# KV transposed by DMA, one weight load split in two, and half-width ones matmuls, in a fused adaLN, linear attention and GEGLU kernel

## The chip, the core and the metric

The kernel runs on one core of a Trainium2 chip. The metric is the device time of one execution in microseconds. Seven of the fast runs show a mean granted clock of TensorE of 0.998 in place of 1.000. A second number is used throughout: the span of one profiled execution and the stretches inside it, which the trace gives to 0.01 us.

Engine names: PE is TensorE (matmuls), PEld its weight loads, DVE is VectorE, ACT is ScalarE, SPq is the queue of SyncE, from which almost all loads and stores are issued.

## The reference, cut to what matters

```python
mod = silu(c) @ w_mod                  # six rows of 1024: sa, ca, ga, sb, cb, gb
h   = layernorm(x) * (1 + ca) + sa     # x: 2048 tokens x 1024
q, k, v = h @ wqkv                     # 32 heads of 32
pq, pk  = phi(q), phi(k)               # phi(t) = (t > 0 ? t + 1 : exp(t)) + 1e-6
kv  = pk^T v  per head                 # 32 x 32
o   = (pq @ kv) / (pq . sum(pk))
x   = x + ga * (o @ wo)
h   = layernorm(x) * (1 + cb) + sb
x   = x + gb * (gelu(h @ w_gate) * (h @ w_up)) @ w_down
```

The kernel never forms `o`. It multiplies KV by wo first (called W2 below), scales pq by the reciprocal of the denominator, and multiplies the scaled pq by W2.

## The kernel before

Four heads form a group, so KV is eight masked blocks of 128x128 (`KVBD`). The product with wo needs each block transposed as the stationary operand: eight PE transposes into PSUM bank 4, then a copy by ScalarE.

```python
def kvt():
    for g in range(NG):                                    # NG = 8
        e.transpose(PS16(4, g*P, (g+1)*P), KVBD[:, g, :], IDENT)    # PE
    e.activation(KVT, PS16(4), Copy)                                # ACT

def w2_pair(g, b0=2):                  # one wo product: two matmuls, banks b0 and b0 + 1
    for half in range(2):
        e.matmul(PS(b0 + half), KVT[:, g, :], WO[:, g, half*512:(half+1)*512])
    e.activation(W2[:, g, :], both banks, Copy)
```

A Q block is eight matmuls of 512 columns into one PSUM bank. Its bank is free once `phi` is through with it: ScalarE takes the exponential, VectorE does two more passes, the last of which ("pq addition") reads the bank again.

```python
def phi(bank, dst):
    e.activation(EB, PS(bank), Exp)                        # ACT
    e.tensor_scalar(EB, EB, 1.0, 1e-6, min, add)           # DVE
    e.scalar_tensor_tensor(dst, PS(bank), 0.0, EB, max, add)   # DVE: the pq addition

def q_next():
    b = (0, 1, 2, 3)[n] if n < 4 else n % 2                # n counts these Q blocks
    q_block(..., b)

den(0, 3)          # denominators; DVE: add, reciprocal; store to DRAM
rb_load(0); rb_load(1)   # 16 loads that spread the reciprocals over the partitions ("rb")
kvbd()             # DVE masks KV
q_next(); q_next()
for u in range(8):
    q_next()
    if u == 0: kvt()
    else:      w2_pair(u - 1)
    if u in (3, 4): pq_scale(0, 0, GH[u - 3])    # DVE: pq times rb, first half of the tokens
    if u in (6, 7): pq_scale(0, 1, GH[u - 6])
w2_pair(7, 4)
# ... then 12 wo chunks (pq times W2), the FFN
```

The rows of `mod` that vary along the free dimension are made by matmuls with a stationary operand of ones, 32 columns wide. Row j lands in partitions 32j to 32j+31:

```python
for h in range(2):                     # high and low half of the value
    for j in range(n):                 # n = 2 or 4 rows of 512
        e.matmul(ps_all[32*j:32*(j+1), bank], ONES, src(k0 + j, h))
```

At the start, the first 25 us, loads of x, of four quarters of w_mod ("wmq") and of wk arrive in turns. A quarter of w_mod has to be multiplied before the k matmuls of the matching two 128-row pieces of wk can use their input. wk's second quarter comes in one load, the third and fourth in two each.

Of the kernel before, what the change touches and what calls it, by code (L numbers as in the profile page):

```python
# [7 lines left out]
ACTF = mybir.ActivationFunctionType  # L8
ALU = mybir.AluOpType

P = 128
# [7 lines left out]
NG = 8  # L19
# [195 lines left out]
def bass_adaLN_cond__linear_attn_block__geglu_ffn__prompt_kernel(  # L215
# [13 lines left out]
    scr_row = nc.dram_tensor("scr_row", [3, 4, 512], f32).ap()  # L229
    scr_rd = nc.dram_tensor("scr_rd", [NSG, 2, HPG, NG * (SGW // 2)], f32).ap()  # L230
    with ExitStack() as es:
# [3 lines left out]
        ps_all = es.enter_context(nc.psum_tensor("ps_all", [P, 8 * 512], f32))  # L235
        ps16 = ps_all.bitcast(bf16)

        def at(name, shape, dty, off):
            return nc.alloc_sbuf_tensor_at(name, shape, dty, offset=ABASE + off, align_bytes=4)
# [45 lines left out]
        KVBD = at("kvbd", [P, NG, P], bf16, OFF_ROW)  # L285
        KVT = at("kvt", [P, NG, P], bf16, OFF_ROW + 2048)
# [22 lines left out]
        IDENT, BMASK, BM32, Z32 = (_small[k] for k in ("ident", "bmask", "bm32", "z32"))  # L309
        RDC = _small["rdc"]  # L310
        ONES, SILF, C8, CT, CHALF, THC, SILUT = (_small[k] for k in ("ones", "silf", "c8", "cT", "chalf", "thc", "siluT"))
# [5 lines left out]
        def r_sm(name):  # L317
            return [(SMO[name], SMO[name] + SMSZ[name], name)]
# [68 lines left out]
        def r_kvbd(g0, g1):  # L387
            return [(OFF_ROW + g0 * 256, OFF_ROW + g1 * 256, "kvbd")]

        R_KVT = [(OFF_ROW + 2048, OFF_ROW + 4096, "kvt")]  # L390

        def pr(b):
            return [(b * 2048, (b + 1) * 2048)]
# [4 lines left out]
        def PS16(b, c0=0, c1=1024):  # L398
            return ps16[:, b * 1024 + c0: b * 1024 + c1]

        sch = Sched()
        T, A, V, G, Q = PE_, ACT_, DVE_, POOL_, SP_
# [11 lines left out]
        def pset_writer(b, o):  # L414
            for t_ in pr(b):
                sch.ps.set_writer(t_[0], t_[1], o)
# [30 lines left out]
        def w_dma(dst, off, name, kind, c0, c1, dc0=0, dc1=NDC):  # L447
            return sch.dma(Q, lambda e: e.dma_start(dst[:, dc0:dc1, c0:c1], wqkv_v[:, dc0:dc1, kind * D + c0:kind * D + c1]),  # L448
                           wr=[t_ for dc in range(dc0, dc1) for t_ in r_w(off, name, dc, c0, c1)], note=f"{name}.{dc0}.{c0}")

        def wmq_dma(q, ts=(0, 1)):
            for t in ts:
                sch.dma(Q, lambda e, t=t: e.dma_start(WMQ[q][:, :, t, :], wm_v[:, :, t * D + q * 256:t * D + (q + 1) * 256]),  # L453
                        wr=r_wmq(q, t), note=f"wmq{q}.{t}")
# [10 lines left out]
        x_dma(3, 4)  # L465
        for q in range(1, 4):
            wmq_dma(q)
            for d0, d1 in ((2, 4),) if q == 1 else ((2 * q, 2 * q + 1), (2 * q + 1, 2 * q + 2)):
                w_dma(WK, OFF_WK, "wk", 1, 0, D, d0, d1)
        w_dma(WV, OFF_WV, "wv", 2, 0, 512, 0, 4)  # L470
        w_dma(WV, OFF_WV, "wv", 2, 0, 512, 4, 8)
# [7 lines left out]
               rd=r_sm("c8") + r_sm("ident"), pwr=pr(4))  # L479
# [4 lines left out]
               rd=r_sm("thc") + r_sm("chalf"), wr=r_sm("siluT"))  # L484
# [68 lines left out]
        def tdma(stream, dst, src, rng, wr_, note):  # L553
            d_ = [last_t[0]] if last_t[0] is not None and last_t[0].stream != stream else []
            last_t[0] = sch.dma(stream, lambda e: e.dma_start_transpose(out=dst, in_=src), rd=rng, wr=wr_, deps=d_, note=note)
# [81 lines left out]
        def mod_rows(parts):  # L637
            for k0, n, bank, src in parts:
                o = None
                for h in range(2):  # L640
                    for j in range(n):
                        ap, rng = src(k0 + j, h)
                        o = sch.op(T, lambda e, h=h, j=j, ap=ap, bank=bank: e.matmul(  # L643
                            ps_all[32 * j:32 * (j + 1), bank * 512:(bank + 1) * 512], ONES[:, :], ap, start=(h == 0), stop=(h == 1)),
                            rd=rng + r_sm("ones"), pwr=(pr(bank) if h == j == 0 else ()), note=f"modr{k0}.{h}.{j}")
                pset_writer(bank, o)

        def mod_store(n, bank, dst, rng, row):
            sch.op(A, lambda e: e.activation(dst[0:32 * n, :], ps_all[0:32 * n, bank * 512:(bank + 1) * 512], ACTF.Copy),
                   prd=pr(bank), wr=rng, note=f"mrow{row}")  # L650
            return sch.dma(Q, lambda e: e.dma_start(scr_row[row, 0:n, :], dst[0:32 * n:32, :]), rd=rng, note=f"mrow{row}.st")

        def hl_src(k, h):
            return HL[k // 4][:, k % 4, h, :], r_hl(k, h, h + 1)
# [184 lines left out]
        for c_ in range(4):  # L839
            for vc, jg in (((0, 0), (1, 0)), ((0, 1), (1, 1)), ((2, 0), (2, 1)), ((3, 0), (3, 1)))[c_]:  # L840
                b = nb()
# [58 lines left out]
        for c_ in range(4, NCH):  # L900
# [23 lines left out]
            for jg in range(2):  # L924
                b = nb()
# [3 lines left out]
            for jg in range(2):  # L929
                b = nb()  # L930
# [3 lines left out]
            if c_ == 13:  # L934
# [6 lines left out]
                for dst, nt, a0 in ((SBT, "sbT", 0), (CBT, "cbT", 2)):  # L941
                    sch.dma(Q, lambda e, dst=dst, a0=a0: e.dma_start(dst[:, :], scr_row[1, a0:a0 + 2, :].rearrange("a (b p) -> p (a b)", p=P)),
                            wr=r_sm(nt), deps=[o_r], note=nt)
# [13 lines left out]
        def kvbd():  # L957
            for kb, gs in ((5, [0, 1, 2]), (6, [3, 4, 5]), (7, [6, 7])):
                n = len(gs)
                src = ps_all[:, kb * 512: kb * 512 + n * KV_SLOT].rearrange("p (a b) -> p a b", a=n)[:, :, 0:P]  # L960
                sch.op(V, lambda e, src=src, gs=gs, n=n: e.tensor_tensor(
                    KVBD[:, gs[0]:gs[0] + n, :], src, BMASK[:, :].unsqueeze(1).to_broadcast([P, n, P]), ALU.mult),
                    prd=pr(kb), rd=r_sm("bmask"), wr=r_kvbd(gs[0], gs[0] + n), note=f"kvbd{kb}")

        def kvt():
            for g in range(NG):
                sch.op(T, lambda e, g=g: e.transpose(PS16(4, g * P, (g + 1) * P), KVBD[:, g, :], IDENT[:, :]),
                       rd=r_kvbd(g, g + 1) + r_sm("ident"), pwr=pr(4), note=f"kvT{g}")
            sch.op(A, lambda e: e.activation(KVT[:].rearrange("p a b -> p (a b)"), PS16(4), ACTF.Copy), prd=pr(4), wr=R_KVT, note="kvt")

        def w2_pair(g, b0=2):
            for half in range(2):
                b = b0 + half
                sch.op(T, lambda e, b=b, half=half: e.matmul(PS(b), KVT[:, g, :], WO[:, g, half * 512:(half + 1) * 512], start=True, stop=True),  # L974
                       rd=R_KVT + [(OFF_WS + g * 2048 + half * 1024, OFF_WS + g * 2048 + (half + 1) * 1024, "wo")], pwr=pr(b), note=f"w2 {g}.{half}")
            sch.op(A, lambda e: e.activation(W2[:, g, :], ps_all[:, b0 * 512:(b0 + 2) * 512], ACTF.Copy),
                   prd=pr(b0) + pr(b0 + 1), wr=r_w(OFF_WK, "w2", g), note=f"w2cp{g}")
# [3 lines left out]
        def den(pr_, b):  # L981
            o = None
            for g in range(NG):
                for i in range(4):
                    sg, t0 = 2 * pr_ + i // 2, (i % 2) * HW
                    o = sch.op(T, lambda e, g=g, i=i, sg=sg, t0=t0: e.matmul(  # L986
                        ps_all[32 * i:32 * (i + 1), b * 512:b * 512 + HW], Z32[:, g, :], PQ[sg][:, g, t0:t0 + HW],
                        start=(g == 0), stop=(g == NG - 1)),
                        rd=r_sm("z32") + r_pq(sg, g, g + 1, t0, t0 + HW), pwr=(pr(b) if g == 0 else ()), note=f"den{pr_} {g}.{i}")
            pset_writer(b, o)  # L990
            sch.op(V, lambda e: e.tensor_scalar(RDC[:, :], PS(b, 0, HW), 1e-6, None, op0=ALU.add), prd=pr(b), wr=r_sm("rdc"), note=f"dene{pr_}")
            sch.op(V, lambda e: e.reciprocal(RDC[:, :], RDC[:, :]), rd=r_sm("rdc"), wr=r_sm("rdc"), note=f"rden{pr_}")
            o_s = sch.dma(Q, lambda e: e.dma_start(scr_rd[2 * pr_:2 * pr_ + 2].rearrange("s f k (g t) -> (s f k g) t", g=NG), RDC[:, :]),
                          rd=r_sm("rdc"), note=f"rden{pr_}.st")
            o_rd[pr_] = o_s
# [4 lines left out]
        def rb_load(sg):  # L1000
            i = sg % 2
            for h in range(2):
                made = []
                for k in range(HPG):
                    made.append(sch.dma(Q, lambda e, h=h, k=k: e.dma_start(
                        RB[i][32 * k:32 * (k + 1), h, :, :].rearrange("p a b -> p (a b)"),
                        scr_rd[sg, h, k:k + 1, :].to_broadcast([32, NG * HW])),
                        wr=r_rb(i, h) if k == 0 else (), deps=made[0].deps if k else [o_rd[sg // 2]], note=f"rb{sg}.{h}.{k}"))
                rb_ops[sg, h] = made
# [24 lines left out]
        q_evac(*first_q)  # L1034
        q_next()
        den(0, 3)
        rb_load(0)
        rb_load(1)
        kvbd()
        q_next()  # L1040
        q_next()
        for u in range(NG):
            q_next()
            if u == 0:
                kvt()
            else:
                w2_pair(u - 1)
            if u in (3, 4):
                pq_scale(0, 0, GH[u - 3])
            if u in (6, 7):  # L1050
                pq_scale(0, 1, GH[u - 6])
# [265 lines left out]
```

## Time and profile before

| | before |
|---|---|
| time, median of 6 runs beside the changed kernel | 838.81 us (837.82 to 840.23) |
| span of the profiled run | 835.7 us |
| PE busy | 829.8 us |
| waits of PE after the first 31 us | none |

The page of the profile, first the busy time of PE and then the chain that ended last, by engine:

```profile
PE 829.8 (99%) x4189; PEld 384.2 (46%) x4189; DVE 512.3 (61%) x898; ACT 336.2 (40%) x555; POOL 36.7 (4%) x91
...
PE 97%; SPq 2%; DMA 1%; issue 0%; DVE 0%
```

PE's waits over the whole span (line that waited, what it waited for, us in total, times, longest). All three lie in the first 25 us:

```profile
PE ps_all L478 <- POOL bmask L429: 2.1, 1, 2.1
PE ps_all L602 <- DMA wmq<-in_w_mod_dram: 0.6, 2, 0.4
PE ps_all L680 <- DVE h1T L565: 0.5, 1, 0.5
```

The chain of work that ended last, in order of time (start, us, what). L602 is the product that reads the last wmq quarter, L643 the ones matmuls, L986 the denominators, L721 Q blocks, L967 the KV transposes, L974 wo products, L1072 the wo chunks, L1157 the FFN's last matmuls:

```profile
24.78 0.95 PE ps_all L602 x32
...
151.80 0.97 PE ps_all L643 x12
...
173.68 0.99 PE ps_all L986 x32
174.67 5.29 PE ps_all L721 x24
179.96 0.45 PE ps_all L967 x8
180.40 1.73 PE ps_all L721 x8
182.13 0.43 PE ps_all L974 x2
182.56 1.73 PE ps_all L721 x8
...
195.94 3.45 PE ps_all L1072 x16
...
348.98 0.54 PE ps_all L643 x4
349.52 48.45 PE ps_all L1157 x224
...
784.75 48.50 PE ps_all L1157 x280
```

Read it as a ledger. From 24.78 us to the end, each piece begins where the one before it ends, so every microsecond taken off PE there is a microsecond of span, unless PE then meets a wait. The candidates of this change are the 0.45 us of transposes and the two sets of ones matmuls, 0.97 and 0.54 us. One Q block is 1.73 us, one wo product 0.43. VectorE starts the first scaling with the spread reciprocals at 188.24 us.

Two lines of the timeline of VectorE show how near other waits are. The columns are start, us, engine, line, operation, out<-in, forms:

```profile
181.37 0.69 DVE L672 SCALAR_TENSOR_TENSOR pq<-ps_all,eb 128x512 bf16<-128x512 f32 x1
...
188.24 1.28 DVE L1018 TENSOR_TENSOR pq<-pq,rb 128x512 bf16<-128x512 bf16 x2
```

The first is the pq addition that frees bank 0 at 182.06 us; the Q block that writes bank 0 next starts at 182.56 in the chain: half a microsecond of slack. The second is the first scaling with the spread reciprocals.

### The profile page before, as it was taken

What the parts mean: (1) busy time and instruction counts of PE and PEld (TensorE: products, weight loads), DVE (VectorE), ACT (ScalarE), POOL (GpSimd) and SP (SyncE); (2) the same over time, 40 slices, a digit from 0 to 9 for tenths busy, and PEclk for the clock granted to TensorE, in tenths of its full rate; (3) what the DMA queues carried; (4) which work ended last, traced back from release to release, by engine and by line L of the source; (5) the groups of instructions that cost most, each with busy time, mean ns of one, the idle gap of its engine ahead of it and who ended that gap; (6) DMA issues with size and microseconds to landing.
All of it is one profiled execution on the core that took longest, in us unless ns stands there. A gap on an engine that the chain in (4) does not pass through costs nothing.

```text
span 835.7 us, 11352 instructions
## 1 busy us (share of the span) xinstructions
PE 829.8 (99%) x4189; PEld 384.2 (46%) x4189; DVE 512.3 (61%) x898; ACT 336.2 (40%) x555; POOL 36.7 (4%) x91
## 2 busy tenths in 40 slices
PE   8999999999999999999999999999999999999998
PEld 4544444444444444444444444444444444444445
DVE  6778877687785567753566665355556535555512
ACT  2357777446423354420444442045554104455300
POOL 2012111000200000000000000000000000000000
PEclk9999999999999999999999999999999999999999
DMA  9984323239796779180555533055553305555000
GB/s 284 332 240 120 83 76 84 70 88 227 151 234 194 227 210 275 26 188 26 158 151 151 152 101 75 20 158 152 151 151 102 76 20 161 153 154 143 7 19 26
DMA packets 184102, 113.22 MB, mean 135 GB/s; under 512 B 35560, under 2 KB 175080, under 8 KB 183024
## 3 DMA queue, kind: packets, MB, share of 16 engines
q1 hardware_dynamic: 184032, 112.50, 49.9%
q8 instruction: 33, 0.54, 0.3%
q14 instruction: 21, 0.17, 0.1%
q10 hardware_dynamic: 16, 0.00, 0.0%
HBM read 100.67 MB, written 4.47 MB: 126 GB/s over the span
## 4 chain that ended last, share of the span: by engine, by line
PE 97%; SPq 2%; DMA 1%; issue 0%; DVE 0%
PE ps_all L1157 23%; PE ps_all L1129 23%; PE ps_all L1132 23%; PE ps_all L680 12%; PE ps_all L1072 7%; PE ps_all L721 7%; SPq L448 1%; PE ps_all L702 1%; SPq L453 1%; DMA wmq<-in_w_mod_dram 1%; PE ps_all L974 0%; PE ps_all L986 0%; SPq L442 0%; PE ps_all L643 0%; PE ps_all L756 0%; PE ps_all L602 0%
## 5 line engine op out<-in xcount | busy, mean ns | idle before, releaser
L1129 PE MATMUL ps_all<-h2T,wg 128*128 128x512 bf16 x896 | 339.6, 379 | 0.0
L1132 PE MATMUL ps_all<-h2T,wu 128*128 128x512 bf16 x896 | 339.6, 379 | 0.0
L1157 PE MATMUL ps_all<-wd,yT 128*128 128x512 bf16 (+3 forms) x952 | 194.2, 366 | 0.0
L1140 ACT ACTIVATE q<-ps_all 128x512 f32<-128x512 f32 x112 | 66.9, 597 | 226.1 <-PE ps_all L1129 222.2
L1157 PEld LDWEIGHTS ps_all<-wd,yT 128*128 128x128 bf16 x952 | 90.1, 98 | 103.9 <-issue 0.4
L1129 PEld LDWEIGHTS ps_all<-h2T,wg 128*128 128x128 bf16 x896 | 87.7, 98 | 105.8 <-issue 0.2
L1132 PEld LDWEIGHTS ps_all<-h2T,wu 128*128 128x128 bf16 x896 | 87.7, 98 | 105.6
L1145 DVE SCALAR_TENSOR_TENSOR ww<-th,guh 128x512 f32<-128x512 f32 x112 | 77.5, 692 | 77.9 <-ACT th L1144 77.9
L1142 DVE SCALAR_TENSOR_TENSOR ww<-q,ps_all 128x512 f32<-128x512 f32 x112 | 76.9, 687 | 77.5 <-ACT guh L1141 77.5
L1144 ACT ACTIVATE th<-ww 128x512 f32<-128x512 f32 x112 | 70.5, 629 | 87.4 <-DVE ww L1142 87.4
L1162 DVE TENSOR_TENSOR ps_all<-ps_all,gbb 128x512 f32<-128x512 f32 (+3 forms) x34 | 22.7, 667 | 94.8 <-PE ps_all L1157 94.8
L1147 DVE TENSOR_TENSOR yT<-ww,ps_all 128x512 bf16<-128x512 f32 x112 | 76.9, 686 | 3.8
L1141 ACT ACTIVATE guh<-ps_all 128x512 f32<-128x512 f32 x112 | 66.2, 591 | 0.0
L721 PE MATMUL ps_all<-h1T,wq 128*128 128x512 bf16 x256 | 58.7, 379 | 0.0
L680 PE MATMUL ps_all<-wv,h1T 128*128 128x512 bf16 x256 | 57.7, 379 | 0.0
L669 ACT ACTIVATE eb<-ps_all 128x512 f32<-128x512 f32 x64 | 37.5, 599 | 49.7 <-PE ps_all L721 22.1
L680 PE MATMUL ps_all<-wk,h1T 128*128 128x512 bf16 x248 | 56.6, 379 | 0.5 <-DVE h1T L565 0.5
L1072 PE MATMUL ps_all<-w,pq 128*128 128x512 bf16 x256 | 56.2, 379 | 0.0
L670 DVE TENSOR_SCALAR eb<-eb 128x512 f32<-128x512 f32 x64 | 27.1, 424 | 26.4 <-ACT eb L669 26.0
L1072 PEld LDWEIGHTS ps_all<-w,pq 128*128 128x128 bf16 x256 | 25.0, 98 | 30.2 <-issue 0.2
L680 PEld LDWEIGHTS ps_all<-wv,h1T 128*128 128x128 bf16 x256 | 24.9, 98 | 29.5
L680 PEld LDWEIGHTS ps_all<-wk,h1T 128*128 128x128 bf16 x248 | 23.8, 98 | 28.8 <-DVE h1T L565 1.6
(96 smaller groups left out, 479.7 us busy)
## 6 DMA issues: line engine op xcount, KB each, us to landing
wg<-in_B_w_gate_dram SPq DMA_DIRECT2D x56, 512.0 KB, 4.1
wu<-in_B_w_up_dram SPq DMA_DIRECT2D x56, 512.0 KB, 5.3
rb<-scr_rd SPq DMA_DIRECT2D x32, 256.0 KB, 7.4
wd<-in_B_w_down_dram SPq DMA_DIRECT2D x7, 1024.0 KB, 8.7
wmst<-in_w_mod_dram SPq DMA_DIRECT2D x6, 1024.0 KB, 6.7
wmq<-in_w_mod_dram SPq DMA_DIRECT2D x8, 512.0 KB, 6.8
out_dram<-xall SPq DMA_DIRECT2D x31, 128.0 KB, 1.7
xall<-in_A_x_dram SPq DMA_DIRECT2D x3, 1024.0 KB, 11.9
```

The lines of the kernel that those rows point to most:

```text
L680: o = sch.op(T, lambda e, dc=dc: e.matmul(PS(bank), H1[sg][:, dc, ci * P:(ci + 1) * P], W_[:, dc, jg * 512:(jg + 1) * 512], start=(dc == 0 ...
L721: o = sch.op(T, lambda e, dc=dc: e.matmul(PS(b), WQ[:, dc, qc * P:(qc + 1) * P], H1[sg][:, dc, :], start=(dc == 0), stop=(dc == NDC - 1)), ...
L1072: last[half] = sch.op(T, lambda e, g=g, half=half: e.matmul(PS(b0 + half), PQ[sg][:, g, ci * P:(ci + 1) * P], W2[:, g, half * 512:(half + ...
L1129: og = sch.op(T, lambda e, dc=dc: e.matmul(PS(bg), WG[slot][:, dc, e_ * P:(e_ + 1) * P], H2[sg][:, dc, :], start=(dc == 0), stop=(dc == ND ...
L1132: ou = sch.op(T, lambda e, dc=dc: e.matmul(PS(bu), WU[slot][:, dc, e_ * P:(e_ + 1) * P], H2[sg][:, dc, :], start=(dc == 0), stop=(dc == ND ...
L1140: sch.op(A, lambda e: e.activation(Q1[j][:, :], PS(bg), ACTF.Square, scale=math.sqrt(GELU_A)), prd=pr(bg), wr=rq, note=f"q1 {fc}")
L1141: ogh = sch.op(A, lambda e: e.activation(GUH[j][:, :], PS(bg), ACTF.Copy, scale=0.5), prd=pr(bg), wr=rg, note=f"gh {fc}")
L1142: sch.op(V, lambda e: e.scalar_tensor_tensor(WW[j][:, :], Q1[j][:, :], 1.0, PS(bg), op0=ALU.add, op1=ALU.mult), rd=rq, prd=pr(bg), wr=rw, ...
L1144: sch.op(A, lambda e: e.activation(TH[j][:, :], WW[j][:, :], ACTF.Tanh, scale=GELU_C), rd=rw, wr=rt, note=f"th {fc}")
L1145: sch.op(V, lambda e: e.scalar_tensor_tensor(WW[j][:, :], TH[j][:, :], 1.0, GUH[j][:, :], op0=ALU.add, op1=ALU.mult), rd=rt + rg, wr=rw, n ...
L1147: sch.op(V, lambda e: e.tensor_tensor(YT[:, fc, :], WW[j][:, :], PS(bu), ALU.mult), rd=rw, prd=pr(bu), wr=r_yt(fc), note=f"yT {fc}")
L1157: o = sch.op(T, lambda e, b=b, fc=fc, c0=c0, c1=c1, n=n: e.matmul(PS(b, 0, n), YT[:, fc, ci * P:(ci + 1) * P], WDT[fc // 4][:, fc % 4, c0:c1],
```

## The change

The intent is to take work off PE. (1) One DMA transposes KV, in place of eight PE transposes and a ScalarE copy. Since a DMA takes longer to arrive (3.3 us from issue to landing in the changed kernel), each wo product moves one Q block later, and two of them follow the seventh block of the loop. (2) For two-row results, each row of 512 is cut in two halves of 256, so that four 32-column groups of the array work instead of two. (3) The second quarter of wk comes in two loads.

```diff
-            for d0, d1 in ((2, 4),) if q == 1 else ((2 * q, 2 * q + 1), (2 * q + 1, 2 * q + 2)):
+            for d0, d1 in ((2 * q, 2 * q + 1), (2 * q + 1, 2 * q + 2)):
                 w_dma(WK, OFF_WK, "wk", 1, 0, D, d0, d1)
 # ... in mod_rows, with w = n * P:
-                    for j in range(n):
-                        ap, rng = src(k0 + j, h)
-                        ... ps_all[32 * j:32 * (j + 1), bank * 512:(bank + 1) * 512], ONES[:, :], ap
+                    for j in range(4):
+                        ap, rng = src(k0 + j * n // 4, h)
+                        ap = ap[:, j * w % 512:j * w % 512 + w]
+                        ... ps_all[32 * j:32 * (j + 1), bank * 512:bank * 512 + w], ONES[:, :], ap
 # ... (mod_store reads and stores the new layout)
         def kvt():
-            for g in range(NG):
-                sch.op(T, lambda e, g=g: e.transpose(PS16(4, g * P, (g + 1) * P), KVBD[:, g, :], IDENT[:, :]), ...)
-            sch.op(A, lambda e: e.activation(KVT..., PS16(4), ACTF.Copy), ...)
+            tdma(Q, KVT[:, :, :], KVBD[:, :, :].rearrange("p a b -> p (a b)"), r_kvbd(0, NG), R_KVT, "kvT")
 # ... in the loop:
         den(0, 3)
+        kvbd()
+        kvt()
         rb_load(0)
         rb_load(1)
-        kvbd()
         q_next()
         q_next()
         for u in range(NG):
             q_next()
-            if u == 0:
-                kvt()
-            else:
-                w2_pair(u - 1)
+            if u >= 2:
+                w2_pair(u - 2 + (u == 7))
+            if u == 6:
+                w2_pair(5, 4)
```

More of the change, by code (lines that the diff above doesn't have):

```diff
@@ L639, in mod_rows @@
                 o = None
+                w = n * P
                 for h in range(2):
-                    for j in range(n):
-                        ap, rng = src(k0 + j, h)
-                        o = sch.op(T, lambda e, h=h, j=j, ap=ap, bank=bank: e.matmul(
-                            ps_all[32 * j:32 * (j + 1), bank * 512:(bank + 1) * 512], ONES[:, :], ap, start=(h == 0), stop=(h == 1)),
+                    for j in range(4):
+                        ap, rng = src(k0 + j * n // 4, h)
+                        ap = ap[:, j * w % 512:j * w % 512 + w]
+                        o = sch.op(T, lambda e, h=h, j=j, ap=ap, bank=bank, w=w: e.matmul(
+                            ps_all[32 * j:32 * (j + 1), bank * 512:bank * 512 + w], ONES[:, :], ap, start=(h == 0), stop=(h == 1)),
                             rd=rng + r_sm("ones"), pwr=(pr(bank) if h == j == 0 else ()), note=f"modr{k0}.{h}.{j}")
@@ L648, in mod_store @@
         def mod_store(n, bank, dst, rng, row):
-            sch.op(A, lambda e: e.activation(dst[0:32 * n, :], ps_all[0:32 * n, bank * 512:(bank + 1) * 512], ACTF.Copy),
+            w = n * P
+            sch.op(A, lambda e: e.activation(dst[:, 0:w], ps_all[:, bank * 512:bank * 512 + w], ACTF.Copy),
                    prd=pr(bank), wr=rng, note=f"mrow{row}")
-            return sch.dma(Q, lambda e: e.dma_start(scr_row[row, 0:n, :], dst[0:32 * n:32, :]), rd=rng, note=f"mrow{row}.st")
+            return sch.dma(Q, lambda e: e.dma_start(scr_row[row, 0:n, :].rearrange("a (h b) -> (a h) b", b=w), dst[0:128:32, 0:w]), rd=rng, note=f"mrow{row}.st")
         def hl_src(k, h):
@@ L965, in kvt @@
         def kvt():
-            for g in range(NG):
-                sch.op(T, lambda e, g=g: e.transpose(PS16(4, g * P, (g + 1) * P), KVBD[:, g, :], IDENT[:, :]),
-                       rd=r_kvbd(g, g + 1) + r_sm("ident"), pwr=pr(4), note=f"kvT{g}")
-            sch.op(A, lambda e: e.activation(KVT[:].rearrange("p a b -> p (a b)"), PS16(4), ACTF.Copy), prd=pr(4), wr=R_KVT, note="kvt")
+            tdma(Q, KVT[:, :, :], KVBD[:, :, :].rearrange("p a b -> p (a b)"), r_kvbd(0, NG), R_KVT, "kvT")
         def w2_pair(g, b0=2):
```

## The prediction

> **What bounds the kernel.** TensorE. The page gives PE 829.8 us busy of a span of 835.7; the chain of waits is 97% PE. After the first 31 us the table of PE waits names no wait at all; the back-to-back pace is 0.216 us per 512-column matmul (16 in 3.45 us). So only removed PE time, or a new PE wait, can move the span. The first 25 us are bound by loads: PE restarts at 20.57 and 24.78 us, each time for the product that reads a w_mod quarter ("wmq") just landed.
>
> **What the change does, costed from the trace.**
> 1. KV transpose. Removed from PE: 8 transposes, 0.45 us on the chain (179.96 to 180.40). Removed from ScalarE: one 1.02 us copy, not on the chain. Added: one DMA transpose; the twelve of the first layernorm land a median 3.1 us after issue and hold the queue 1.24 us. KV is ready at about 178.9 us, so it lands near 182; the first wo product, one Q block later, needs it near 183.2. No PE wait there.
> 2. Half-width ones matmuls. The four 512-column matmuls of a two-row result use two of the four 32-column groups; eight of 256 columns use four. The Trainium skill (TensorEngine Tiling (Array Packing), Key Properties) says that different tiles run in parallel; the trace agrees: 32 denominator matmuls of 256 columns over four groups take 0.99 us, 0.031 each, against 0.108 for 256 columns at the pace above. The two-row set (0.54 us at 349 us) should take about 0.33. It occurs twice (152 and 349 us): 0.2 us each, 0.4 in all.
> 3. wk rows in two loads. That load lands at 16.9 us and PE starts on it at 17.0, about 0.3 us after its other input. Two loads may start PE earlier there, but PE then waits for wmq at 20.57 and 24.78 anyway, and no bytes are saved. 0, give or take 0.3.
>
> Removed from the chain: about 0.85 us.
>
> **What gives some back.** The DMA transpose goes ahead of the 16 loads of the spread reciprocals ("rb"). They land one per 1.2 us, bound by the DMA engines. The first four are in at 187.6 us and VectorE reads them at 188.24: a slack of 0.6. The transpose delays them by about 0.8 us, while the new order brings VectorE's need forward by about 1.1 us. So I expect a VectorE wait of about 1 us at the first scaling of pq. It delays the Q evacuations behind it; Q blocks alternate between two PSUM banks with about 0.6 us of slack, so PE should stall 0 to 0.5 us near 190 us. Later rb sets have 2 us or more, or fall where PE has other banks.
>
> **Sum.** -0.45 -0.4 +0.3 = about -0.6 us, under 0.1% of the time and below its own scatter (838.2 to 840.2).
>
> Predicted 838.7 us, 8 in 10 between 837.2 and 840.2. Chances: faster by over 2% 0.01, within 2% 0.98, slower by over 2% 0.01.
>
> **What would show each step.** PE's waits: none for the transposed KV; a new short wait of Q matmuls on VectorE near 190 us. VectorE's waits: about 1 us on rb, where there is none now. Groups: transposes of KV and its copy gone; the two-row sets near 0.33 us. Start: the last wmq product still begins near 24.8 us. FFN: unchanged, same pace.
>
> **What would make it wrong.** The DMA transpose landing late (with loads in the queue some took 5 to 8 us): PE would wait for KV by 1 to 4 us. Loads of the start arriving in another order and moving the wmq landings by a microsecond. One more DMA shifts all later loads to other completion lanes; if one then waits behind a slow one, a stall could appear in the FFN. None of these reaches 2%.

## The result, and the profile after

Six runs each: 838.12 us median (837.6 to 838.4) against 838.81 (837.82 to 840.23). The ratio is 0.9989, with a 95% interval of 0.9976 to 1.0002: the same. Ratios in this document are the mean time of one kernel's fast runs over the mean of the other's of the same rounds, so not quite the ratio of the medians. Yet the span of the profiled run is 836.0 us, 0.3 longer than before. The page, as above:

```profile
PE 828.2 (99%) x4189; PEld 383.2 (46%) x4189; DVE 512.4 (61%) x898; ACT 334.7 (40%) x554; POOL 36.7 (4%) x91
...
PE 96%; SPq 2%; DMA 1%; DVE 0%; issue 0%
```

PE is busy for 1.6 us less, and the span is not shorter. The Trainium skill (Perfetto Trace Analysis, the note at its top) warns that matmul busy time is a bad metric for how close a kernel is to its roofline, because matmuls are pipelined. In comparing these two pages it misleads too, for a reason that the traces show: 1.2 of the 1.6 us fall in the first 25 us (21.57 us busy before, 20.36 after), where PE waited longer for loads in this execution, and 0.52 are the new wait below. So the waits and the chain have to be read instead. PE's waits, all of them:

```profile
PE ps_all L478 <- POOL bmask L429: 2.1, 1, 2.1
PE ps_all L602 <- DMA wmq<-in_w_mod_dram: 1.8, 3, 1.2
PE ps_all L724 <- DVE pq L675: 0.5, 1, 0.5
PE ps_all L546 <- DVE xh L505: 0.4, 1, 0.4
PE ps_all L683 <- DVE h1T L565: 0.2, 1, 0.2
```

The third line is new and the only one after the start. The chain (lines moved by a few: L645 ones matmuls, L724 Q blocks, L1073 wo chunks, L1158 the FFN's last matmuls):

```profile
25.23 0.95 PE ps_all L602 x32
...
152.25 0.77 PE ps_all L645 x16
...
173.93 0.99 PE ps_all L986 x32
174.92 2.93 PE ps_all L724 x13
...
181.61 0.70 DVE pq L675
182.45 1.89 PE ps_all L724 x8
184.34 0.43 PE ps_all L974 x2
...
196.43 3.45 PE ps_all L1073 x16
...
349.47 0.33 PE ps_all L645 x8
349.80 48.45 PE ps_all L1158 x224
...
785.02 48.50 PE ps_all L1158 x280
```

The ones matmuls fell from 0.97 to 0.77 and from 0.54 to 0.33 us, and the transposes are gone. But between 174.92 and 182.45 us the chain leaves PE: it passes through the KV mask and three evacuations on VectorE. The moment itself, in the timeline, with the idle time and its releaser in brackets:

```profile
181.61 0.69 DVE L675 SCALAR_TENSOR_TENSOR pq<-ps_all,eb 128x512 bf16<-128x512 f32 x1
...
182.45 0.38 PE L724 MATMUL ps_all<-h1T,wq 128*128 128x512 bf16 x1 [0.52 <-DVE pq L675]
```

This is the third Q block of the loop (u = 2). It writes bank 0, which the first block of the loop wrote before it.

To compare executions, cut the chain at four points: the last wmq product (24.78 before), the denominators (173.68), the first wo chunk (195.94), the first of the FFN's last matmuls (349.52), and the end of the last matmul of the chain (784.75 + 48.50 = 833.25). Before, the four stretches are 148.90, 22.26, 153.58 and 483.73 us, together 808.47. After, they are 148.70, 22.50, 153.37 and 483.72, together 808.29. So the change took 0.20 + 0.21 us off the stretches with the ones matmuls, added 0.24 us where the transposes were removed, and the net is 0.18 us. The 0.45 us later start of the last wmq product (25.23 against 24.78) more than hides that in this pair of spans.

### The profile page after: what moved, and what is told of

Same layout as the page of the kernel before. It is cut to its first block, busy times and chain, and to the rows that moved or that the text cites. A ratio compares the mean times of both kernels' runs of the same rounds, so it can differ in the third digit from the quotient of the medians.

```text
span 836.0 us, 11356 instructions
## 1 busy us (share of the span) xinstructions
PE 828.2 (99%) x4189; PEld 383.2 (46%) x4189; DVE 512.4 (61%) x898; ACT 334.7 (40%) x554; POOL 36.7 (4%) x91
## 4 chain that ended last, share of the span: by engine, by line
PE 96%; SPq 2%; DMA 1%; DVE 0%; issue 0%
PE ps_all L1158 23%; PE ps_all L1130 23%; PE ps_all L1133 23%; PE ps_all L683 12%; PE ps_all L1073 7%; PE ps_all L724 6%; SPq L448 1%; PE ps_all L705 1%; SPq L453 1%; DMA wmq<-in_w_mod_dram 1%; PE ps_all L974 0%; PE ps_all L986 0%; SPq L442 0%; DVE kvbd L964 0%; DVE eb L673 0%
## 5 line engine op out<-in xcount | busy, mean ns | idle before, releaser
L1158 PE MATMUL ps_all<-wd,yT 128*128 128x512 bf16 (+3 forms) x952 | 194.2, 366 | 0.0
L1158 PEld LDWEIGHTS ps_all<-wd,yT 128*128 128x128 bf16 x952 | 90.1, 98 | 103.7 <-issue 0.2
L724 PE MATMUL ps_all<-h1T,wq 128*128 128x512 bf16 x256 | 58.5, 379 | 0.5 <-DVE pq L675 0.5
L1073 PE MATMUL ps_all<-w,pq 128*128 128x512 bf16 x256 | 56.2, 379 | 0.0
L1073 PEld LDWEIGHTS ps_all<-w,pq 128*128 128x128 bf16 x256 | 25.0, 98 | 30.2 <-issue 0.2
L724 PEld LDWEIGHTS ps_all<-h1T,wq 128*128 128x128 bf16 x256 | 24.3, 98 | 27.9 <-issue 1.2
```

The source lines that it names most:

```text
L724: o = sch.op(T, lambda e, dc=dc: e.matmul(PS(b), WQ[:, dc, qc * P:(qc + 1) * P], H1[sg][:, dc, :], start=(dc == 0), stop=(dc == NDC - 1)), ...
L1073: last[half] = sch.op(T, lambda e, g=g, half=half: e.matmul(PS(b0 + half), PQ[sg][:, g, ci * P:(ci + 1) * P], W2[:, g, half * 512:(half + ...
L1158: o = sch.op(T, lambda e, b=b, fc=fc, c0=c0, c1=c1, n=n: e.matmul(PS(b, 0, n), YT[:, fc, ci * P:(ci + 1) * P], WDT[fc // 4][:, fc % 4, c0:c1],
```

## The experiments

Theory D: removing the transposes brings PE to the third Q block of the loop before bank 0 is free, so the saving turns into a wait for the evacuation. Rival E, the prediction's own: the wait comes from the spread reciprocals, held up behind the DMA transpose. For the start: theory A, its variation is chance; rival B, the extra load delays wmq.

All runs in one table. The columns are the stretches just defined, read from each run's chain.

| run | last wmq product starts | to denominators | to first wo chunk | to FFN's last matmuls | to the end | sum |
|---|---|---|---|---|---|---|
| before | 24.78 | 148.90 | 22.26 | 153.58 | 483.73 | 808.47 |
| after | 25.23 | 148.70 | 22.50 | 153.37 | 483.72 | 808.29 |
| wk_only | 24.70 | 148.91 | 22.26 | 153.57 | 483.73 | 808.47 |
| half_only | 24.96 | 148.70 | 22.26 | 153.37 | 483.73 | 808.06 |
| kv_only | 26.39 | 150.60 | 22.49 | 153.58 | 483.73 | 810.40 |
| kv_again | 24.89 | 148.91 | 22.49 | 153.58 | 483.73 | 808.71 |
| bank4 | 25.72 | 148.70 | 21.98 | 153.37 | 483.73 | 807.78 |
| bank4_pq1, best_again | 25.34, 25.37 | 148.70 | 21.84 | 153.37 | 483.73 | 807.64 |
| lag1 | 24.94 | 148.70 | 22.64 | 153.38 | 483.72 | 808.44 |
| half_recip (wrong result) | 25.18 | 148.70 | 22.28 | 153.37 | 483.72 | 808.07 |
| before_again | 24.96 | 148.91 | 22.26 | 153.57 | 483.73 | 808.47 |

Some expectations quote the stretches from the first matmul of one piece to the first of the next, as the trace has their starts; that gives 22.17 for 22.26 and 808.26 for 808.47 of the kernel before, so 0.1 and 0.2 us less than the chain's. That of kv_only also leaves out the 0.99 us of the denominators.

### Each part alone

wk_only is the first hunk of the diff on the kernel before, half_only the second (`mod_rows`, `mod_store`), kv_only the rest (the cuts are shortened):

```diff
-            for d0, d1 in ((2, 4),) if q == 1 else ((2 * q, 2 * q + 1), (2 * q + 1, 2 * q + 2)):   # wk_only
+            for d0, d1 in ((2 * q, 2 * q + 1), (2 * q + 1, 2 * q + 2)):
-                    for j in range(n):                                                             # half_only
+                    for j in range(4):              # ... and the narrower slices
-            if u == 0: kvt()                                                                       # kv_only
-            else:      w2_pair(u - 1)
+            if u >= 2: w2_pair(u - 2 + (u == 7))
+            if u == 6: w2_pair(5, 4)                # ... and the DMA transpose ahead of rb_load
```

> The kernel before with the wk load of the second quarter in two, nothing else. In the profile after, the last wmq product began at 25.23 us, before at 24.78. Theory A: that 0.45 us is chance (when the loads of the start happen to land varies from execution to execution by some tenths); then this run's last wmq product begins anywhere between 24.5 and 25.4, and the timed ratio to before is 1.000 within 0.0007. Rival B: the extra load pushes the wmq landings back; then it begins near 25.2 again, and the time is 0.3 to 0.6 us longer than before. Rival C: the split makes the start more even; then its runs scatter less than those of before (1 us against 2.4) and the mean is up to 1 us shorter. The PE chain from 31 us on is that of before to 0.1 us, whichever holds.

Measured: 838.21 us median against 838.31 of the kernel before, ratio 0.9998 (0.9985 to 1.001). The last wmq product started at 24.70 us, and everything after it is as before.

> The kernel before with the half-width ones matmuls alone. Theory: the two-row set takes 0.33 us in place of 0.54 where it stands alone (FFN), the twelve-row-matmul set of 0.97 us becomes sixteen in 0.77, and from the last wmq product to the last matmul the chain is 0.41 us shorter than before. Rival: the 0.2 us near 152 us is lost again at the next wait of PE on VectorE (the Q block after the first wo product waits for the evacuation of its bank), so only 0.2 us of 0.4 reach the end. Time: 0.2 to 0.4 us shorter, inside the scatter.

Measured: 837.53 us, ratio 0.999 (0.9978 to 1.0003). The two stretches are 0.20 and 0.21 us shorter, 0.41 together, and the stretch between them is unchanged at 22.26. All of the saving reached the end; the rival falls.

> The kernel before with the KV transpose by DMA and the products one Q block later, alone. Theory D: PE loses 0.45 us of transposes, and the wo product no longer stands between the second and the third Q block of the loop (0.43 us less there), so PE reaches the third Q block 0.9 us earlier than before, while the bank that it writes is freed by VectorE at the same time as before, because VectorE is still behind with reciprocal and KV mask: a PE wait of about 0.7 us on the pq addition, as in the profile after; from the start of the denominator matmuls to the first wo chunk 21.3 to 21.5 us, against 22.26 minus 0.99 = 21.27 before, so the part alone saves nothing or costs 0.2 us. Rival E (my prediction): the wait comes from the loads of the spread reciprocals held up by the DMA transpose, on VectorE at the first scaling of pq; then that wait, about 1 us, shows in VectorE's waits, and PE waits near 190 us, not at the third Q block.

Measured: 838.37 us, ratio 1.0 (0.9986 to 1.0013). Its profiled execution is odd: 841.42 us, granted clock 0.998, and 1.7 us longer in a stretch that the part does not touch. Its trace shows where that went. The granted clock is 0.60, 0.50, 0.50 and 0.70 in the four microseconds from 28 to 32 us, and 1.00 in those on both sides. The 18 k matmuls that run there take 5.59 us, against 3.91 in the kernel before (first line: before; second: kv_only):

```profile
25.73 3.91 PE ps_all L680 x18
27.34 5.59 PE ps_all L680 x18
```

Worked out from these clocks, the dip costs about 4.0 - 2.3 = 1.7 us (an estimate), which is all of it. What set it off is not shown. The five times average 839.03 us with this execution and 838.44 without it; the nine of the kernel before average 838.44. So the part was profiled again:

> The KV part alone once more, since its first profile fell in an execution with a granted clock of 0.998 and is 1.7 us long between the last wmq product and the denominator matmuls, where it has no change. Expected: that stretch 148.83 us as before, the next, up to the first wo chunk, 22.4 (it was 22.41), and from the last wmq product to the last matmul 808.5, so 0.2 us longer than before.

Measured (one run of 838.24 us): 148.91, then 22.49. PE's one wait after the start is again 0.52 us on the pq addition at the third Q block of the loop. The part alone makes its own stretch 0.23 us longer. Theory D's numbers hold. Rival E's wait on rb, 1.3 us, is in this trace too, but at 243.6 us, in the next stretch, which is no longer for it (153.58).

Together: 0.00 for the split load, -0.41 for the half-width matmuls, +0.24 for KV. Their sum, -0.17, is the -0.18 of the whole change.

### One bank for the third Q block

```diff
-            b = (0, 1, 2, 3)[qn[0]] if qn[0] < 4 else qn[0] % 2
+            b = (0, 1, 2, 3, 0, 1, 4)[qn[0]] if qn[0] < 7 else qn[0] % 2
```

> The changed kernel with one number altered: the third Q block of the loop writes PSUM bank 4, which the DMA transpose left free, in place of bank 0. No work and no DMA changes. Theory D: the PE wait of 0.52 us (0.7 us lost) at that block disappears; then PE runs 0.7 us ahead, the first scaling of pq is wanted near 187.6 us, before the reciprocals have landed (188.2 by the spacing of 1.2 us), so VectorE waits some 0.6 us there as predicted, and PE gets 0 to 0.2 us of it; the first wo chunk starts 0.5 to 0.7 us earlier than in the profile after, counted from the start of the denominator matmuls (21.9 in place of 22.50). Rival F: PE's wait is only labelled so and has to do with the DMA transpose itself (landing of KV); then the wait stays, moved to the wo product behind it. Time: 0.5 us shorter than the changed kernel.

Measured: the wait at the third Q block is gone, and the stretch is 21.98 us in place of 22.50. No instruction was added and no DMA moved, so the wait was for the bank; rival F falls. Time 837.53 us, ratio to before 0.9991 (0.9979 to 1.0004). And now what the prediction had expected appears, in the timeline of this run:

```profile
188.63 1.29 DVE L1018 TENSOR_TENSOR pq<-pq,rb 128x512 bf16<-128x512 bf16 x2 [0.42 <-DMA rb<-scr_rd]
...
191.04 0.11 PEld L724 LDWEIGHTS ps_all<-h1T,wq 128*128 128x128 bf16 x2 [0.46 <-DVE pq L675]
```

VectorE waits 0.42 us for the spread reciprocals, and a Q block at 191.04 us has its weight load held up for a bank that VectorE frees late; 0.13 us of that reaches the chain (that Q block takes 1.86 us there in place of 1.73).

### The first scaling one Q block later as well

```diff
-            if u in (3, 4):
-                pq_scale(0, 0, GH[u - 3])
+            if u in (4, 5):
+                pq_scale(0, 0, GH[u - 4])
```

> The bank 4 version, with the first two scalings of pq moved one Q block later. In the bank 4 run VectorE waited 1.1 us for the spread reciprocals (0.42 of it at the first scaling) and PE lost 0.46 us at a Q block near 191 us. If that PE wait is paid for the late reciprocals, then with the scaling one block later VectorE waits under 0.3 us for them, PE has no wait above 0.2 us between the denominator matmuls and the first wo chunk, and that stretch takes 22.17 - 0.45 = 21.7 us (bank 4: 21.88; changed kernel: 22.40; before: 22.17). If instead PE's wait comes from VectorE having too much to do there (four scalings in four blocks), it stays at 0.3 us or more. From the last wmq product to the last matmul: 807.4 us against 808.26 before, all of the expected 0.86.

Measured: the stretch is 21.84 us, 22.26 - 0.42, and PE has no wait after the start. Part of the expectation was wrong: VectorE still waits 1.07 us on rb. That is at 242.6 us, on the fourth set, and was 0.71 of the 1.1 us of the bank 4 run; it costs PE nothing (153.37). The time was no shorter: 838.37 us over six runs, ratio 1.0002 (0.9989 to 1.0015), with single runs from 837.16 to 839.97. Three of the six (839.09, 839.13 and 839.97) are at a granted clock of 0.998. The other three average 837.41 us, against 838.22 for the ten runs of the kernel before at 1.000 (an eleventh was at 0.998): 0.81 us less, near the 0.83 of the stretches, but three runs are few. So it was run once more, with the kernel before as its own control:

> A control: the kernel before, unchanged. Its stretches after the last wmq product must be those of the first profile to 0.02 us (148.90, 22.26, 153.58, 483.73; 808.47 together), and that product may begin anywhere between 24.6 and 25.8 us. The timed ratio to before is that of a kernel to itself: 1.000, with an interval of about 0.0013 to each side, which shows what differences the times can't resolve.

> The version with bank 4 and the later scaling once more. Theory: its stretches after the last wmq product repeat to 0.02 us (148.70, 21.84, 153.37, 483.73; 807.64 together, 0.83 us under before), while when that product begins varies by a microsecond from execution to execution and is not the change's doing. So the ratio is 0.999 when both kernels get the same starts, and the ratio of 1.0002 of the first time was chance. Rival: the version has a later start of its own (its extra load); then that product begins at 25.3 us or later again, and the ratio is 1.000 again.

Measured: the control against itself gave 0.9994 (0.9982 to 1.0007) and the same stretches. The version gave 837.68 us, ratio 0.9986 (0.9972 to 1.0; two of the nine runs of the kernel before were at a clock of 0.998, and without them the difference of the means is 0.64 us), and the same stretches as the first time:

```profile
25.37 0.95 PE ps_all L602 x32
...
174.07 0.99 PE ps_all L986 x32
175.06 8.74 PE ps_all L724 x40
183.79 0.43 PE ps_all L974 x2
...
195.91 3.45 PE ps_all L1073 x16
```

Five Q blocks now run without a break (8.74 us). The version is 0.83 us under the kernel before and 0.65 under the changed kernel, by the sums of the table.

### What the wait for the bank is made of

lag1 puts the wo products back one Q block earlier, with the DMA transpose kept:

```diff
-            if u >= 2:
-                w2_pair(u - 2 + (u == 7))
-            if u == 6:
-                w2_pair(5, 4)
+            if u >= 1:
+                w2_pair(u - 1)
```

> The changed kernel with the wo products at their old place, one Q block earlier than in the change. Theory: PE reaches the first of them 7.9 us after the denominator matmuls began, near 181.75 us of the profile after, but the transposed KV landed at 182.54 there: PE waits about 0.8 us on the DMA, the third Q block then finds its bank free, and the stretch to the first wo chunk is 22.5 us, as in the changed kernel (22.40) within 0.2: the later placement trades the wait for KV against the wait for the bank and wins about 0.1. If the landing were hidden, the stretch would be 21.7.

```profile
178.93 3.32 DMA kvt<-kvbd
182.30 0.61 PE ps_all L974 x2
```

Measured: the chain goes through the transpose, and the stretch is 22.64 us (time 838.06, ratio 0.9997, 0.9985 to 1.0009). The later placement in the change was right about the landing; it only exchanged that wait for one of 0.14 us less.

half_recip takes the reciprocal ahead of the evacuations over half its columns:

```diff
-            e.reciprocal(RDC[:, :], RDC[:, :])
+            e.reciprocal(RDC[:, 0:HW // 2 if pr_ == 0 else HW], same)
```

> The changed kernel with the first reciprocal over half of its columns: wrong result on purpose. It takes 0.85 us off VectorE ahead of the KV mask and of three evacuations of Q blocks. Theory D (the third Q block waits because VectorE is behind): PE's wait of 0.52 us at that block is gone, the transpose and the spread reciprocals start 0.85 us earlier too, and the stretch from the denominator matmuls to the first wo chunk is 21.7 to 21.8 us. If the wait has another cause than VectorE's backlog, the stretch stays near 22.4.

Measured (one run, 837.91 us): 22.28, so only 0.22 of the 0.6 to 0.7 us expected came back, and PE still waited 0.30 us. The chain shows why:

```profile
174.87 5.30 PE ps_all L724 x24
180.25 0.61 ACT eb L672
180.88 0.44 DVE eb L673
181.34 0.70 DVE pq L675
182.18 1.89 PE ps_all L724 x8
```

VectorE is no longer behind here; it starts at once when ScalarE has the exponential. From the end of the first Q block of the loop (180.17) to the start of the block that reuses its bank (182.18) lie 2.01 us: exponential, two VectorE passes and the handovers. One Q block between the two uses covers 1.73. So theory D was half right: of the 0.66 us lost in the changed kernel (22.50 against 21.84), 0.22 came from VectorE's backlog and about 0.44 from the evacuation being longer than the one Q block that hides it. Before the change, the transposes and the first wo product happened to stand in that gap (0.45 + 0.43 us) and filled it.

### Is the start any different?

Across eleven profiles (all but the odd one), time minus start of the last wmq product minus sum of stretches is 4.62 to 4.69 us, 4.66 on average. So a timed run tells its own start, as long as its stretches are those of the table. For the runs at a granted clock of 0.998 that can't be taken for granted: in the one of them that was profiled, the odd one, 1.7 us were lost after the start. All seven took 839.09 us or more. They are left out here, and so are the first six runs of the kernel before, whose clocks are not on record. Over the other timed runs this gives 25.15 us on average for kernels with the wk load in two (30 runs, standard error 0.08) and 25.10 us for kernels with it in one (41 runs, 0.06), while single runs go from 24.55 to 26.28; the standard deviation is 0.41 us in both groups. Rival B falls, and so does a steadier start (rival C): the split does nothing that these runs can resolve. What makes the start vary was not examined.

## Why the prediction was right or wrong

- **The time** (838.7, between 837.2 and 840.2): 838.12, inside. The predicted difference of -0.6 us is near that of the two medians, -0.69, but that is chance: the part that does not vary with the start is -0.18. Three of the six runs of the kernel before took 839.39 us or more, with no clock on record; none of the changed kernel did.
- **PE is the bound, and only PE time or a new PE wait counts**: right. All stretches repeat to 0.02 us and add up, the one with the dip of the clock excepted.
- **Transposes worth 0.45 us**: right as to what was removed. bank4_pq1 keeps 0.42 of it.
- **The landing of the DMA transpose**: right. It took 3.3 us, and no wait of PE on it appears in the changed kernel.
- **Half-width matmuls worth 0.2 us twice**: right, 0.20 and 0.21, shown alone. The Trainium skill's statement that different tiles run in parallel (TensorEngine Tiling (Array Packing), Key Properties) agrees with it: 0.54 us became 0.33 for the same 2048 columns.
- **The split load worth nothing**: right. wk_only's last wmq product started at 24.70, and 71 runs show no difference of the start.
- **The give-back: this step failed.** The prediction put it as a VectorE wait of about 1 us at the first scaling of pq, because the reciprocals come later, and a PE stall of 0 to 0.5 us near 190 us. In the changed kernel VectorE has no wait on rb at all. PE lost 0.66 us, where the sum had allowed 0.3, at the third Q block of the loop, at 182.45 us, waiting for a bank. The prediction took one slack, about 0.6 us, for all Q blocks, and never asked what the block has that loses the transposes and the wo product in front of it: there the bank was free only 0.50 us before its use, of which the handover takes 0.14 (182.31 to 182.45), and PE came 0.88 us earlier. That makes the wait of 0.52 us; the rest is in the block itself, which takes 1.89 us in the chain in place of 1.73. That first stall also put off the need for the reciprocals until they had landed. With it removed (bank4), the predicted chain of waits appears where it was said, at 0.42 us on VectorE and 0.13 on PE's chain.

## What to carry to other kernels

Work that looks like pure cost on the busiest engine can be the filler that hides a neighbour's latency: before removing it, ask for each wait that stands just behind it how much slack is left, block by block, not on average. With two banks in turn, what stands between two uses of a bank must last as long as its whole evacuation (2.0 us here); a third bank is the cheap remedy, and removing an operation may itself free one. When a change is worth less than the scatter of the times, cut the chain at fixed points and compare the stretches: here they repeat to 0.02 us while the times spread over 2 us. Look at the granted clock of each run first: a dip of four microseconds cost one execution 1.7 us, over twice what the best version gains.

## What the Trainium skill lacked or had wrong

- VectorE: DVE Perf Modes, "The three transpose paths", gives 1309 ns for one 128x128 bf16 transpose by DMA and 390 ns on TensorE; its "Rules for kernel authors" advise TensorE where PSUM will do. The page has no figure for several tiles at once; other pages give bandwidths of DMA transposes, but none the time from issue to landing of one of this size. Here eight tiles in one DMA took 3.3 us from issue to landing and held the queue 1.28 us, and eight back to back on PE took 0.45 us of the chain: neither is eight times the page's figure.
- Perfetto Trace Analysis, "Matmuls" (under "Optimizing Tensor Performance"), says that independent matmul groups should rotate through different PSUM banks so that evacuation overlaps the next matmuls. A later section, "Matmul Optimizations", asks that all 8 banks be used. Neither says how long an evacuation a given number of banks can hide. Here two banks and blocks of 1.73 us lost 0.44 us to an evacuation of 2.01 us, and a third bank for one block removed it.
- No page gives a figure for how far the time of a whole kernel varies between executions. Here, on one core, the stretches after the loads of the start repeated to 0.02 us between profiled runs that share them (one execution of twelve, with a dip of the clock, excepted), while the start, worked out from 71 times at a granted clock of 1.000, varied between 24.55 and 26.28 us.
